# A linear-attention and two-MLP kernel on one core: when layer 1's weight sums and stores are issued, and the last eight attention chunks in halves of 64 tokens

## The chip, the cores and the metric

The kernel runs on one core of one Trainium2 chip. Times are device microseconds (us) of one execution. TensorE (PE in the profile) does the matrix products; VectorE (DVE) and ScalarE (ACT) do the arithmetic between them; SyncE (SP) issues nearly all DMA transfers, in the order in which they are written, on one queue. The metric is the median time over several runs.

## The reference, cut to what matters

Causal linear attention with a decay per head, then two MLPs without biases, all in float32:

```python
# q, k, v: (4, 8, 768, 64)
gamma = 1.0 - 2.0 ** (-5.0 - np.arange(H))
for t in range(S):
    state = gamma * state + einsum('bhd,bhe->bhde', k[:, :, t], v[:, :, t])
    y[:, :, t] = scale * einsum('bhd,bhde->bhe', q[:, :, t], state)
x = y.transpose(0, 2, 1, 3).reshape(3072, 512)
h = x @ w_in;  x = (h * sigmoid(1.702 * h)) @ w_out      # w_in (512, 2048)
h = x @ w_in2; out = (max(h, 0) + alpha * min(h, 0)) @ w_out2
```

## The kernel before, in words

**Precision.** A float32 product is made of three products of rounded parts. A tensor is split into a high part, rounded by a cast on ACT, and a low part, the remainder, subtracted on DVE (`g_split`, `piece_hi`/`piece_lo` at L223 to L229, `x_split`).

**Two stages.** The 3072 tokens make six blocks of 512, or 24 attention chunks of 128 (six chunks to a sequence). The first stage does blocks 0 and 1 through MLP layer 1 by plain products: 32 steps, each an `mlp_h` of 12 matmuls into `ph` (L661) and an `mlp_y` of 12 matmuls into `py` (L680) that stands one step later (LAG = 1), so the last two `mlp_y` follow each other. A step has two *slots*: slot 2s comes behind the `mlp_h` of step s, slot 2s + 1 behind the `mlp_y` that follows it. The second stage (slot 64, called `base`, and later) does everything else, layer 1 of blocks 2 to 5 and all of layer 2, with a scheme of seven products for a 2x2 block product: 280 `h_unit`s of 6 matmuls (`pa` and `pd`, L763) and 280 `y_chunk`s (L836). It needs sums and differences of weight blocks (s1 to s4) and of activation blocks. Slots of the second stage come behind every third or fourth `h_unit`.

**Jobs in slots.** Everything that isn't a step or a unit is a job with a slot, in the dictionary `jobs`; `run(slot)` issues what stands there. On this one stream of work lie:

- `conv_words`, `conv_f32`, `conv_hi`, `conv_lo`: a weight block, given as 64-bit words, becomes a high and a low part. Layer 1's blocks m = 10 to 31 come at slots 11 + 1.1 (m - 10).
- `store` (L251): writes the parts of a block of layer 1 to device memory, at slot 24 + 0.9 (m - 10) for m = 10 to 31.
- `conv_sums` (L264, four DVE instructions on L271) at the slots of `SUMS_IN` (w_in) and, by `slice_sums`, `SUMS_OUT` (w_out); one slot later `conv_split` (L301) casts each sum on ACT (L225), subtracts the rest on DVE (L229) and stores both.
- `x_prep`: blocks of x for the second stage, from slot 53 to 62.

**Attention.** Chunks 0 to 7 and 16 to 23 go whole: `att_scores` (L332) makes the 128x128 scores `sc`, DVE multiplies them by the decay mask (`a`), and one slot later `att_out` (L360) makes the output `px` and the state update `pu`; `att_state` folds `pu` into the running state `diag`, and `att_x_kept` (L434) writes the output's scaled form into the `xl` tiles. Chunks 8 to 15 go in halves of 64 tokens: `half_step(o, new)` (L528), at the slots 36, 38, to 52, makes the scores and state updates of chunk `new` and, between them, the output of chunk `o` from its own scores and from two states, that before the chunk (`hstate`) and that in its middle (`mid`). DVE then makes `a` (L543), `mid` and `hstate` (L557, L561, L562) and `xl` (L572). ACT scales `v` by the decay one slot ahead (`half_v_scale`, L471). Loads of chunks 14 and later come by `load_early` into tiles named `early`. Between the two forms `swap_state` (L459) copies the state by three DMAs, as the halves keep two heads of each pair the other way round.

**What sets the order.** Each engine runs its instructions in program order. The tile framework puts the DVE and ACT instructions of an `mlp_h` or half step ahead of waiting weight work (`tc.high_priority`), by its own estimate and not by what happens on the chip. Each SP DMA also waits for the one eight places ahead of it.

Of the kernel before, what the change touches and what calls it, by code (L numbers as in the profile page):

```python
# [8 lines left out]
F32 = mybir.dt.float32  # L9
# [6 lines left out]
ALU = mybir.AluOpType  # L16
# [3 lines left out]
P = 128  # L20
C = 128
# [9 lines left out]
BT = 512  # L31
NB = NT // BT
LEAD = 5
# [4 lines left out]
HG = 100  # L38
EARLY = (
    {},  # L40
# [3 lines left out]
)  # L44
# [14 lines left out]
AHEAD = 3  # L59
YLAG = 36  # L60
QORD = [(6, 7, 4, 5, 0, 1, 2, 3)] + [tuple(range(8))] * 4
SUMS_IN = (37, 41, 45, 49, 53, 56, 59, 62)
SUMS_OUT = (62, 64, 66, 68, 47, 51, 55, 58)
LOADED = 4
RESIDENT = (6, 7)
RINGED = range(8, 14)
LOADS = (-5, -3, -1, 1, 2, 3, 4, 5)
STORE_W = (24, 0.9)
ATT1 = 36
W2_ORDER = [("in", i) for i in range(6)] + [("out", i) for i in range(4)]  # L70
W2_ORDER += [("in", 6), ("in", 7)] + [("out", i) for i in range(4, 8)]
# [4 lines left out]
def tile_linear_attention_two_mlps(ctx: ExitStack, tc, qk, kv, w1, w2, consts, alpha, out):  # L76
# [9 lines left out]
    nc = tc.nc  # L86
# [9 lines left out]
    ps_y = pool("ps_y", 1, space=PS)  # L96
# [9 lines left out]
    decay_out = cst[:, NLEAD:].rearrange("p (n i) -> p n i", n=NP)  # L106
    alpha_sb = cpool.tile([P, NF], F32, name="alpha_sb")
    nalpha = cpool.tile([P, NF], F32, name="nalpha")
    diag = cpool.tile([P, NP, D], F32, name="diag")
    hstate = [cpool.tile([P, NP, D], F32, name=f"hstate{i}") for i in range(2)]  # L110
# [14 lines left out]
    def take(name, shape=(P, 512), dtype=F32):  # L125
        i = free.popleft()
        t = spool.tile(list(shape), dtype, tag=f"s{i}", name=name)
        home[id(t)] = (i, t)
        return t

    def give(*ts):
        for t in ts:
            free.append(home.pop(id(t))[0])
# [36 lines left out]
    early = {}  # L170
# [147 lines left out]
    def new_x(j):  # L318
        x_hi[j] = xpool.tile([P, NP, BT], F32R, tag=f"xhi{j}", name="xhi")
        x_lo[j] = xpool.tile([P, NP, BT], F32R, tag=f"xlo{j}", name="xlo")  # L320


    att, xl = {}, {}

    def att_psum(c, which, shape):
        early = EARLY[c] if c < BT // C else EARLY[1] if c >= 4 * BT // C else {}
        if which in early:
            tag = early[which]
            return (ps_h if tag == "h" else ps_y).tile(shape, F32, tag=tag, name=which)
        return ps_a.tile(shape, F32, tag="a", name=which)  # L330
# [71 lines left out]
    def att_state(c):  # L402
        first = c % CPB == 0
        att[c], pu = att[c]
        if pu is not None:
            src = pu
            if not first:
                src = take("t", (P, NP, D))
                nc.vector.tensor_tensor(out=src, in0=pu, in1=diag, op=ALU.add)
                give(src)  # L410
            dec = decay_c.unsqueeze(2).to_broadcast([P, NP, D])
            nc.vector.tensor_tensor(out=diag, in0=src, in1=dec, op=ALU.mult)

    def att_x(c):
        if c >= 2 * BT // C:
            att_x_kept(c)
            return
        x32 = take("x32", (P, NP, C))
        early_x = c == BT // C - 1
        banks = att[c][0] if early_x else att[c]  # L420
        for n in range(2):
            px = banks[n][:, :2 * C].rearrange("p (n i) -> p n i", n=2)
            with tc.high_priority(HG):
                nc.vector.tensor_tensor(out=x32[:, n::2, :], in0=px, in1=decay_out[:, n::2, :], op=ALU.mult)
        j, i = divmod(c, BT // C)
        cols = slice(i * C, (i + 1) * C)
        if i == 0:
            new_x(j)
        nc.scalar.copy(out=x_hi[j][:, :, cols], in_=x32)  # L429
        if early_x:  # L430
            att_state(c)
        att[c] = x32

    def att_x_kept(c):  # L434
        banks = att.pop(c)
        t, i = divmod(c % (2 * BT // C), BT // C)
        for k in range(2):
            for d in range(2):
                if i == 0:
                    xl[k, d, t] = take("xl")  # L440
                with tc.high_priority(HG):
                    nc.vector.tensor_tensor(
                        out=xl[k, d, t][:, i * C:(i + 1) * C], in0=banks[k][:, d * C:(d + 1) * C],
                        in1=decay_out[:, 2 * d + k, :], op=ALU.mult,
                    )

    def att_x_low(c):
        j, i = divmod(c, BT // C)
# [12 lines left out]
        for s in range(2):  # L461
            nc.sync.dma_start(out=out[ROWS[s], 0::2, :], in_=src[ROWS[1 - s], 0::2, :])

    def half_psum(which):
        return (ps_h if which == "sc" else ps_a).tile([P, 512], F32, tag="h" if which == "sc" else "a", name=which)

    def half_v_scale(c):
# [53 lines left out]
    def leave(kind, c):  # L521
        loaded.pop((kind, c))
        if c in early:
            give(*early[c][:2] if kind == "qk" else early[c][2:])
        else:
            done()

    def half_step(o, new):  # L528
        if o is not None:
            att["px", o] = half_psum("px")  # L530
        if new is not None:
            att["sc", new] = half_psum("sc")
            att["pu", new] = half_psum("pu")
        half_products(o, new)
        if o is not None:
            give(att.pop(("v", o)), att.pop(("a", o)), att.pop(("mid", o)))
            leave("qk", o)
        if new is not None:
            leave("kv", new)
        with tc.high_priority(HG):  # L540
            if new is not None:
                a = att["a", new] = take("a", (P, 2 * NP, HC))
                nc.vector.tensor_tensor(  # L543
                    out=a, in0=att.pop(("sc", new)).rearrange("p (n i) -> p n i", i=HC),
                    in1=half_causal.unsqueeze(1).to_broadcast([P, 2 * NP, HC]), op=ALU.mult,
                )
                half_state(new)
            if o is not None:
                half_x(o)
# [13 lines left out]

    def half_x(c):
        px = att.pop(("px", c)).rearrange("p (n i) -> p n i", n=NP)
        n = c - 2 * BT // C
        t, i = divmod(n, BT // C)
        for k in range(2):
            for d in range(2):
                if i == 0:  # L570
                    xl[k, d, t] = take("xl")
                nc.vector.tensor_tensor(  # L572
                    out=xl[k, d, t][:, i * C:(i + 1) * C], in0=px[:, 2 * d + k, :],
                    in1=decay_out[:, 2 * d + k, :], op=ALU.mult,
                )
# [319 lines left out]
    per = BT // C  # L895
# [3 lines left out]
    base = 2 * len(steps)  # L899
# [3 lines left out]
    def job(slot, fn, *args, load=()):  # L903
        jobs.setdefault(int(slot), []).append((fn, args, load))

    def attention(c, s_scores, s_out, s_x, s_low):
        if c < 4 * per:
            job(s_scores, att_scores, c, load=(("qk", c), ("kv", c)))
        else:
            job(LOADS[c - 4 * per] + base, load_early, c)  # L910
            job(s_scores, att_scores, c)
        job(s_out, att_out, c)
        job(s_x, att_x, c)
        if c < 2 * per:
            job(s_low, att_x_low, c)

    def convert(key, slot):
        job(slot, conv_words, key, load=(key,))
# [3 lines left out]
        if key[2] % 2 and (key[0] == "in" or key[1] == 2):  # L922
            i = key[2] // 2
            s = slot + 3 if key[1] == 2 else SUMS_IN[i]
            job(s, conv_sums, key[0], key[1], i)
            job(s + 1, conv_split, key[0], key[1], i)

    turn_at = {}
    for c in range(NCH):
        if 2 * per <= c < 4 * per:  # L930
            s = ATT1 + 2 * (c - 2 * per)
            turn_at.setdefault(s, {})["new"] = c
            turn_at.setdefault(s + 2, {})["o"] = c
            if c in RINGED:
                job(s - 1, half_v_scale, c, load=(("qk", c), ("kv", c)))
            else:
                job(s - 4, load_early, c)
                job(s - 1, half_v_scale, c)
            continue
        if c < per:  # L940
            s = 2 * c - 2 * per - 1
        elif c < 2 * per:
            s = 2 * (c - per)
        else:
            s = base + c - 4 * per
        attention(c, s, s + 1, s + 1, s + 2)
    for s, t in turn_at.items():
        job(s, half_step, t.get("o"), t.get("new"))
    job(2 * per + 4, swap_state, hstate[2 * per % 2], diag)
    job(ATT1 + 4 * per, swap_state, diag, hstate[4 * per % 2])  # L950
    for ft in range(NF):
        for n, kind in enumerate(("in", "out")):
            m = 2 * ft + n
            lead = 2 * LEAD
            convert((kind, 1, ft), m - 2 * per + CS if ft < LEAD else lead + 1 + 1.1 * (m - lead))
            kind, i = W2_ORDER[m // 2]
            convert((kind, 2, 2 * i + m % 2), base + W2_AT[m])
            job(12 + m if ft < LEAD else STORE_W[0] + STORE_W[1] * (m - 10), store, (("in", "out")[n], 1, ft))
    for i in range(NQ):
        if i < LOADED:  # L960
            job(SUMS_OUT[i] - 2, slice_load, i)
# [37 lines left out]
    o = NLEAD  # L999
# [172 lines left out]
```

## Time and profile before

| | before |
|---|---|
| runs, us | 1038.05, 1035.78, 1036.85 |
| median, us | 1036.85 |
| profiled execution, span us | 1037.7 |
| PE busy, share of the span | 1019.7 us, 98% |
| DVE busy | 873.8 us, 84% |
| ACT busy | 679.3 us, 65% |
| mean granted TensorE clock, share of full speed | 0.996 |

The profiled execution has no time of its own beside its span of 1037.7 us, from its first to its last instruction; the median of the runs is 0.85 us below it. Shares are averages over both stages. Matmuls are pipelined, so a matmul's duration is not the distance to the next one.

### The profile page before, as it was taken

What the parts mean: (1) busy time and instruction counts of PE and PEld (TensorE: products, weight loads), DVE (VectorE), ACT (ScalarE), POOL (GpSimd) and SP (SyncE); (2) the same over time, 40 slices, a digit from 0 to 9 for tenths busy, and PEclk for the clock granted to TensorE, in tenths of its full rate; (3) what the DMA queues carried; (4) which work ended last, traced back from release to release, by engine and by line L of the source; (5) the groups of instructions that cost most, each with busy time, mean ns of one, the idle gap of its engine ahead of it and who ended that gap; (6) DMA issues with size and microseconds to landing.
All of it is one profiled execution on the core that took longest, in us unless ns stands there. A gap on an engine that the chain in (4) does not pass through costs nothing.

```text
span 1037.7 us, 18658 instructions
## 1 busy us (share of the span) xinstructions
PE 1019.7 (98%) x6316; PEld 837.9 (81%) x6316; DVE 873.8 (84%) x1738; ACT 679.3 (65%) x1405; POOL 0.2 (0%) x4
## 2 busy tenths in 40 slices
PE   7999999898999999999999999999999999999998
PEld 5778888787888888888888888888888888888886
DVE  6999845997989999888899999998677978677792
ACT  6887835466776885765886776775555855556740
POOL 0000000000000000000000000000000000000000
PEclk9999999998999999999999999999999999999999
DMA  8689939689999889989989899896786766775671
GB/s 326 228 266 396 349 118 368 228 320 319 385 392 388 268 310 370 324 309 357 341 286 361 276 320 334 294 314 180 228 274 212 220 215 194 226 245 178 187 203 61
DMA packets 147231, 289.80 MB, mean 279 GB/s; under 512 B 17472, under 2 KB 17856, under 8 KB 147136
## 3 DMA queue, kind: packets, MB, share of 16 engines
q1 hardware_dynamic: 146848, 288.30, 80.8%
q8 instruction: 50, 0.82, 0.3%
q10 hardware_dynamic: 288, 0.31, 0.1%
q14 instruction: 45, 0.37, 0.1%
HBM read 213.83 MB, written 74.45 MB: 278 GB/s over the span
## 4 chain that ended last, share of the span: by engine, by line
PE 85%; DVE 8%; DMA 4%; ACT 1%; SPq 1%; issue 0%; DVEq 0%; ACTq 0%
PE py L836 37%; PE pa L763 21%; PE pd L763 16%; PE py L680 5%; PE ph L661 4%; DMA wcin<-wb 2%; DVE wb L229 1%; PE px L372 1%; DVE s L271 1%; PE sc L344 1%; DMA early<-kv 1%; DVE gl L645 1%; DMA ld<-kv 1%; DVE a L355 1%; DMA early<-qk 1%; DVE cvt L210 0%
## 5 line engine op out<-in xcount | busy, mean ns | idle before, releaser
L836 PE MATMUL py<-gh,yw 128*128 128x512 f32 x1120 | 299.5, 389 | 0.0
L836 PEld LDWEIGHTS py<-gh,yw 128*128 128x128 f32 x1120 | 210.2, 188 | 43.7
L763 PE MATMUL pa<-xo,hw 128*128 128x512 f32 x912 | 231.0, 390 | 0.0
L763 PEld LDWEIGHTS pa<-xo,hw 128*128 128x128 f32 x912 | 170.9, 188 | 35.8
L645 DVE TENSOR_TENSOR gl<-gw,gh 128x512 fp32r<-128x512 f32 x240 | 161.1, 687 | 42.9 <-ACT gh L644 36.9
L644 ACT CAST gh<-gw 128x512 fp32r<-128x512 f32 x240 | 145.7, 620 | 53.6 <-PE py L836 24.3
L763 PE MATMUL pd<-xo,hw 128*128 128x512 f32 x684 | 173.3, 389 | 0.0
L836 PE MATMUL py<-gl,yw 128*128 128x512 f32 x560 | 172.6, 389 | 0.0
L763 PEld LDWEIGHTS pd<-xo,hw 128*128 128x128 f32 x684 | 128.2, 188 | 26.8
L836 PEld LDWEIGHTS py<-gl,yw 128*128 128x128 f32 x560 | 105.1, 188 | 21.8
L850 DVE TENSOR_TENSOR yc<-py,yc 128x512 f32<-128x512 f32 x99 | 63.7, 684 | 26.2 <-PE py L836 26.2
L637 DVE SCALAR_TENSOR_TENSOR gw<-t,nalpha,gw 128x512 f32<-128x512 f32 x96 | 71.4, 748 | 15.5 <-ACT gw L636 15.3
L635 ACT ACTIVATE t<-gw 128x512 f32<-128x512 f32 x72 | 45.5, 632 | 52.7 <-DVE gw L778 49.8
L225 ACT CAST wb<-s 128x256 fp32r<-128x256 f32 x128 | 48.3, 402 | 41.4 <-DVE s L271 27.6
L680 PE MATMUL py<-gh,wb 128*128 128x512 f32 x256 | 67.3, 405 | 3.2 <-ACT gh L644 2.8
L661 PE MATMUL ph<-xhi,wb 128*128 128x512 f32 x256 | 64.2, 392 | 1.2 <-ACT xhi L429 1.2
L775 ACT COPY gw<-pa 128x512 f32<-128x512 f32 x80 | 46.8, 585 | 26.3 <-PE pa L763 25.7
L680 PEld LDWEIGHTS py<-gh,wb 128*128 128x128 f32 x256 | 47.9, 192 | 15.4 <-ACT gh L644 4.1
L661 PEld LDWEIGHTS ph<-xhi,wb 128*128 128x128 f32 x256 | 47.6, 188 | 11.6 <-ACT xhi L429 1.3
L778 DVE TENSOR_TENSOR gw<-pd,gw 128x512 f32<-128x512 f32 x80 | 54.8, 685 | 2.2 <-PE pd L763 2.1
L229 DVE TENSOR_TENSOR wb<-s,wb 128x256 fp32r<-128x256 f32 x128 | 50.0, 419 | 7.1 <-ACT wb L225 6.9
L799 DVE TENSOR_TENSOR gw<-gw 128x512 f32<-128x512 f32 x80 | 53.9, 688 | 0.3
(119 smaller groups left out, 1358.4 us busy)
## 6 DMA issues: line engine op xcount, KB each, us to landing
hw<-wcin SPq DMA_DIRECT2D x266, 256.0 KB, 4.7
yw<-wcout SPq DMA_DIRECT2D x232, 256.0 KB, 3.8
ld<-w SPq DMA_DIRECT2D x64, 512.0 KB, 5.9
wcin<-wb SPq DMA_DIRECT2D x112, 256.0 KB, 5.1
wcout<-wb SPq DMA_DIRECT2D x88, 256.0 KB, 4.2
yw<-wo SPq DMA_DIRECT2D x48, 256.0 KB, 5.1
wo<-wb SPq DMA_DIRECT2D x32, 256.0 KB, 6.3
early<-qk SPq DMA_DIRECT2D x26, 256.0 KB, 6.0
```

The source lines that it names most:

```text
L225: nc.scalar.copy(out=w[:, 0:256], in_=src)
L229: nc.vector.tensor_tensor(out=w[:, 256:], in0=src, in1=w[:, 0:256].bitcast(F32), op=ALU.subtract)
L637: nc.vector.scalar_tensor_tensor(out=g, in0=t, scalar=nalpha[:, ft:ft + 1], in1=g, op0=ALU.mult, op1=ALU.add)
L644: nc.scalar.copy(out=gh, in_=g)
L645: nc.vector.tensor_tensor(out=gl, in0=g, in1=gh.bitcast(F32), op=ALU.subtract)
L661: nc.tensor.matmul(out=ph, lhsT=cols(w, low, k), rhs=x[:, k, :], start=(n == 0), stop=(n == len(prods) - 1),)
L680: nc.tensor.matmul(out=py[e], lhsT=lhsT, rhs=g, start=(begin and seen[e] == 1), stop=(end and seen[e] == 3))
L763: nc.tensor.matmul(out=ps, lhsT=w[:, 256 * part_ + k * P:256 * part_ + (k + 1) * P], rhs=x[2 * k + low], start=(n in (0, 1, 3) and m == 0) ...
L778: nc.vector.tensor_tensor(out=g, in0=ps, in1=g, op=ALU.add)
L799: sub = lambda o, x, y: nc.vector.tensor_tensor(out=o, in0=x, in1=y, op=ALU.subtract)
L836: nc.tensor.matmul(out=ps[e], lhsT=w[:, at:at + P], rhs=t, start=(fresh and seen[e] == 1), stop=(m == GQ - 1 and seen[e] == 3), skip_group ...
L850: add_ = lambda o, x: nc.vector.tensor_tensor(out=o, in0=ps, in1=x, op=ALU.add)
```

## The change

`SUMS_IN` brings the eight `conv_sums` of w_in forward, from slots 37 to 62 to slots 33 to 51. A new `STORE_FAST` leaves the stores alone up to slot 31 and lets those behind it follow 0.4 slot apart instead of 0.9, so that the last comes at slot 36 and not 42. Chunks 16 to 23 go in halves too, by `half_step` at slots `base` to `base + 8`, one slot apart. In that stage the banks of `sc`, `pu` and `px` are those of `ps_y`, as the whole form had them. `att_x_kept`, the second `swap_state` and a use of `EARLY` go.

```diff
-SUMS_IN = (37, 41, 45, 49, 53, 56, 59, 62)
+SUMS_IN = (33, 35, 37, 39, 41, 44, 47, 51)
 SUMS_OUT = (62, 64, 66, 68, 47, 51, 55, 58)
 LOADS = (-5, -3, -1, 1, 2, 3, 4, 5)
 STORE_W = (24, 0.9)
+STORE_FAST = (31, 0.4)
...
 def att_x(c):
-        if c >= 2 * BT // C:
-            att_x_kept(c)
-            return
...
-    def half_psum(which):
+    def half_psum(which, c):
+        if c >= 4 * BT // C:
+            tag = {"sc": f"y{3 * (c % 2)}", "pu": "y1", "px": "y2"}[which]
+            return ps_y.tile([P, 512], F32, tag=tag, name=which)
         return (ps_h if which == "sc" else ps_a).tile([P, 512], F32, tag="h" if which == "sc" else "a", name=which)
...
+    def store_slot(m):
+        s = STORE_W[0] + STORE_W[1] * (m - 2 * LEAD)
+        late = max(0, s - STORE_FAST[0])
+        return min(s, STORE_FAST[0] + late * STORE_FAST[1] / STORE_W[1])
...
     for c in range(NCH):
-        if 2 * per <= c < 4 * per:
-            s = ATT1 + 2 * (c - 2 * per)
+        if c >= 2 * per:
+            late = c - 4 * per
+            s, after = (base + late, 1) if late >= 0 else (ATT1 + 2 * (c - 2 * per), 2)
             turn_at.setdefault(s, {})["new"] = c
-            turn_at.setdefault(s + 2, {})["o"] = c
+            turn_at.setdefault(s + after, {})["o"] = c
             if c in RINGED:
                 job(s - 1, half_v_scale, c, load=(("qk", c), ("kv", c)))
             else:
-                job(s - 4, load_early, c)
+                job(LOADS[late] + base if late >= 0 else s - 4, load_early, c)
                 job(s - 1, half_v_scale, c)
             continue
...
-    job(ATT1 + 4 * per, swap_state, diag, hstate[4 * per % 2])
...
-            job(12 + m if ft < LEAD else STORE_W[0] + STORE_W[1] * (m - 10), store, (("in", "out")[n], 1, ft))
+            job(12 + m if ft < LEAD else store_slot(m), store, (("in", "out")[n], 1, ft))
```

On DVE, the end of the first stage, before: from behind the third-last `gl` of the 32 steps to the last. `s_3344` and `s_3345` are sums of w_in, `s_3356` and `s_3357` of w_out (made from `wsum`).

```order
L271 TENSOR_TENSOR s_3344<-cvt 128x256
L271 TENSOR_TENSOR s_3345<-cvt 128x256
L271 TENSOR_TENSOR s_3344<-s_3344,cvt 128x256
L294 TENSOR_TENSOR wsum<-wo 128x256
L271 TENSOR_TENSOR s_3345<-cvt,s_3344 128x256
L294 TENSOR_TENSOR wsum<-wo 128x256 x2
L601 TENSOR_TENSOR t_3121<-xl,t_3121 128x512
L601 TENSOR_TENSOR t_3131<-xl,t_3131 128x512
L229 TENSOR_TENSOR wb<-s_3344,wb 128x256 x2
L229 TENSOR_TENSOR wb<-s_3345,wb 128x256 x2
L645 TENSOR_TENSOR gl<-g,gh 128x512
L294 TENSOR_TENSOR wsum<-wo 128x256
```

And in the changed kernel, the same place (lines L295, L272, L230 and L632 are what L294, L271, L229 and L645 were, and L576 what L589 was):

```order
L632 TENSOR_TENSOR gl<-g,gh 128x512
L295 TENSOR_TENSOR wsum<-wo 128x256 x3
L272 TENSOR_TENSOR s_3369<-wsum 128x256
L272 TENSOR_TENSOR s_3369<-s_3369,wsum 128x256
L230 TENSOR_TENSOR wb<-s_3369,wb 128x256
L272 TENSOR_TENSOR s_3370<-wsum,s_3369 128x256
L230 TENSOR_TENSOR wb<-s_3369,wb 128x256
L230 TENSOR_TENSOR wb<-s_3370,wb 128x256
L632 TENSOR_TENSOR gl<-g,gh 128x512
L576 TENSOR_TENSOR xo<-xl,xo 128x512 x2
L576 TENSOR_TENSOR xo<-t_3178,xo 128x512
L632 TENSOR_TENSOR gl<-g,gh 128x512
```

The sums of w_in made from `cvt` are gone from this place; the sum of w_out stands ahead of the second-last `gl` and no longer between it and the last.

On ACT, before, around the last activation `g` of the first stage; `wb` are the casts of the sum of w_out.

```order
L632 ACTIVATE g<-ph 128x512
L644 CAST gh<-g 128x512
L225 CAST wb<-s_3356 128x256
L225 CAST wb<-s_3357 128x256
L225 CAST wb<-s_3356 128x256
L225 CAST wb<-s_3357 128x256
L588 CAST xo<-xl 128x512 x2
L632 ACTIVATE g<-ph 128x512
L588 CAST xo<-t_3121 128x512
L644 CAST gh<-g 128x512
```

In the changed kernel, from the second-last `g` to the last:

```order
L619 ACTIVATE g<-ph 128x512
L631 CAST gh<-g 128x512
L459 ACTIVATE v<-early,cst 128x64 x8
L575 CAST xo<-xl 128x512 x2
L619 ACTIVATE g<-ph 128x512
L575 CAST xo<-t_3178 128x512
L631 CAST gh<-g 128x512
```

Ahead of the last `g` stand eight scalings of `v` (chunk 16) where four casts of sums stood.

On PE, the changed kernel's first two attention jobs of the second stage, the first with `new` alone, the second with both; the products of a line pair follow each other in turns, of which the first are shown.

```order
L750 MATMUL pd<-xo,wb 128x512 x12
L469 MATMUL sc<-early 64x64 x16
L469 MATMUL pu<-v,early 64x64 x16
L750 MATMUL pa<-xo,wb 128x512 x12
L750 MATMUL pd<-xo,wb 128x512 x6
L469 MATMUL px<-early,hstate_82 64x64
L469 MATMUL sc<-early 64x64
L469 MATMUL px<-early,hstate_82 64x64
```

Before, the row of `pd` x12 was followed by eight scores of 128x128, and the second job by the 24 or 32 products of `att_out` (x8 of 64x64 into `px` first) and the next chunk's scores. The units between them are the same ones in both kernels.

## Rows read from the trace of the kernel before

**Rows 1.** Timeline of PE, half steps without a wait: start, us, what.

```profile
139.93 1.15 PE L481 MATMUL sc<-ld 64*64 64x64 f32 x32
...
141.94 2.11 PE L680 MATMUL py<-gh,wb 128*128 128x512 f32 x8
...
147.61 0.27 PE L481 MATMUL px<-ld,hstate 64*64 64x64 f32 x1
...
149.63 1.66 PE L680 MATMUL py<-gh,wb 128*128 128x512 f32 x6
```

**Rows 2.** Timeline of PE, starts of the last three half steps and a pause.

```profile
187.11 0.24 PE L481 MATMUL px<-ld,hstate 64*64 64x64 f32 x1 [0.26 <-DVE hstate L561]
...
196.64 0.29 PE L481 MATMUL px<-early,hstate 64*64 64x64 f32 x2 [1.66 <-DVE hstate L561]
...
200.59 0.21 PE L481 MATMUL pu<-v,early 64*64 64x64 f32 x1 [1.85 <-issue]
...
206.52 0.68 PE L481 MATMUL px<-early,hstate 64*64 64x64 f32 x16
```

**Rows 3.** The chain that ended last: start, us, what; a transfer and two units.

```profile
179.41 7.37 DMA early<-kv
...
262.93 2.72 PE pa L763 x12
```

**Rows 4.** Timeline of PE, the end of the first stage.

```profile
235.93 1.98 PE L680 MATMUL py<-gh,wb 128*128 128x512 f32 x8
...
241.65 3.78 PE L680 MATMUL py<-gh,wb 128*128 128x512 f32 x8 [2.84 <-ACT gh L644]
...
246.94 3.29 PE L763 MATMUL pa<-xo,wb 128*128 128x512 f32 x12
250.06 2.88 PE L763 MATMUL pd<-xo,wb 128*128 128x512 f32 x12
```

**Rows 5.** Timeline of ACT at the same place.

```profile
237.29 1.13 ACT L225 CAST wb<-s 128x256 fp32r<-128x256 f32 x3 [3.06 <-DVE s L271]
...
240.98 0.61 ACT L644 CAST gh<-g 128x512 fp32r<-128x512 f32 x1
```

**Rows 6.** Windows: length, PE, PEld, DVE, ACT, POOL busy, PE clock, DMA share, GB/s.

```profile
130.00:140.00 10.00, 10.00 (x47) 8.01 (x47) 3.42 (x7) 4.26 (x13) 0.00 (x0) 1.00 0.00 0
...
190.00:200.00 10.00, 7.09 (x145) 5.82 (x144) 9.68 (x29) 3.90 (x10) 0.00 (x0) 1.00 0.69 236
...
230.00:240.00 10.00, 8.81 (x39) 6.95 (x37) 9.97 (x28) 5.05 (x13) 0.00 (x0) 1.00 0.96 329
240.00:250.00 10.00, 8.35 (x24) 6.67 (x25) 8.12 (x17) 8.02 (x28) 0.00 (x0) 0.66 0.71 239
...
280.00:290.00 10.00, 10.00 (x130) 8.12 (x130) 10.00 (x28) 7.54 (x20) 0.00 (x0) 1.00 1.04 381
```

**Rows 7.** Timeline of PE, whole chunks in the second stage: first two and last.

```profile
252.87 1.16 PE L344 MATMUL sc<-early 64*128 64x128 f32 x16
...
253.96 3.02 PE L763 MATMUL pa<-xo,wb 128*128 128x512 f32 x12
...
258.27 0.69 PE L372 MATMUL px<-v,early 128*64 128x64 f32 x16
...
261.27 0.96 PE L763 MATMUL pd<-xo,wb 128*128 128x512 f32 x3
...
315.40 0.96 PE L763 MATMUL pa<-xo,hw 128*128 128x512 f32 x3
```

**Rows 8.** Timeline of DVE: instructions that follow each other at once.

```profile
189.48 0.42 DVE L271 TENSOR_TENSOR s<-s,wsum 128x256 f32<-128x256 f32 x1
189.82 0.42 DVE L229 TENSOR_TENSOR wb<-s,wb 128x256 fp32r<-128x256 f32 x1
...
219.35 0.68 DVE L645 TENSOR_TENSOR gl<-g,gh 128x512 fp32r<-128x512 f32 x1
219.96 0.68 DVE L589 TENSOR_TENSOR xo<-t,xo 128x512 fp32r<-128x512 f32 x1
```

More of the change, by code (lines that the diff above doesn't have):

```diff
@@ L325, in att_psum @@
     def att_psum(c, which, shape):
-        early = EARLY[c] if c < BT // C else EARLY[1] if c >= 4 * BT // C else {}
+        early = EARLY[c] if c < BT // C else {}
         if which in early:
@@ L432, in att_x @@
         att[c] = x32
[L434 to L445, printed above, removed]
     def att_x_low(c):
@@ L529, in half_step @@
         if o is not None:
-            att["px", o] = half_psum("px")
+            att["px", o] = half_psum("px", o)
         if new is not None:
-            att["sc", new] = half_psum("sc")
-            att["pu", new] = half_psum("pu")
+            att["sc", new] = half_psum("sc", new)
+            att["pu", new] = half_psum("pu", new)
         half_products(o, new)
@@ L565, in half_x @@
         px = att.pop(("px", c)).rearrange("p (n i) -> p n i", n=NP)
-        n = c - 2 * BT // C
-        t, i = divmod(n, BT // C)
+        t, i = divmod(c % (2 * BT // C), BT // C)
         for k in range(2):
@@ L906, in attention @@
     def attention(c, s_scores, s_out, s_x, s_low):
[L907 to L911, printed above, removed]
+        job(s_scores, att_scores, c, load=(("qk", c), ("kv", c)))
         job(s_out, att_out, c)
         job(s_x, att_x, c)
-        if c < 2 * per:
-            job(s_low, att_x_low, c)
+        job(s_low, att_x_low, c)
     def convert(key, slot):
@@ L936, in tile_linear_attention_two_mlps @@
             else:
-                job(s - 4, load_early, c)
+                job(LOADS[late] + base if late >= 0 else s - 4, load_early, c)
                 job(s - 1, half_v_scale, c)
             continue
[L940 to L945, printed above, removed]
+        s = 2 * c - 2 * per - 1 if c < per else 2 * (c - per)
         attention(c, s, s + 1, s + 1, s + 2)
@@ L1140, in chosen @@
         n = np.arange(NCH)[:, None, None]
-        return np.where((n >= 2 * BT // C) & (n < 4 * BT // C), half, whole)
+        return np.where(n >= 2 * BT // C, half, whole)
     def weights(w_in, w_out, swap):
```

## The prediction

> **What bounds the kernel now.** The busy times of the page come first: PE is busy 98% of the span, so a gain must be PE work that goes away or a gap on PE that closes. The list of PE's waits and the windows say where the gaps are. In the second stage there are none worth naming: PE is busy 10.00 us of 10, though DVE is full there too (window 280 to 290) [rows 6]. The gaps lie between 180 and 250 us, at the end of the first stage, where DVE is busy 9.68 and 9.97 of 10 and PE 7.09 and 8.81 [rows 6]. The timeline of PE then gives each gap its place.
>
> A half step that waits for nothing takes 2.01 to 2.02 us to the next matmul (139.93 to 141.94, 147.61 to 149.63), and the distance to the next half step is 147.61 - 139.93 = 7.68 us [rows 1]. Eight such distances would put the ninth half step at 139.93 + 61.44 = 201.37. It starts at 206.52 [rows 2]: **5.15 us** are lost. Of these 1.85 lie between 187.11 and 196.64 (mostly the wait of 1.66 for `hstate`), 2.20 between 196.64 and 206.52 (a pause of 1.85 whose releaser the profile does not name), and 1.10 ahead of 187.11 [rows 2], where the chain runs through a late load of keys and values, 7.37 us from issue to landing [rows 3].
>
> The last `mlp_y` waits **2.84 us** for `gh` [rows 4]. `gh` is cast at 240.98, behind an ACT that had itself been waiting 3.06 us for sums of DVE [rows 5]: four casts of a sum stand ahead of the last `g` in ACT's order. So a DVE that is late with weight work holds the one PE step that has no other work to put in front. [...] Twelve matmuls from 241.65 to 246.94 take 5.29 us and the next twelve 3.12 (to 250.06), where the chain has 2.72 for twelve at the full clock [rows 3]. The clock costs 2.57 + 0.40 = **2.97 us** [rows 4].
>
> **The change part by part.**
>
> *Sums of w_in earlier.* Nothing is added or removed. One sum with its split is eight DVE instructions of 128x256, which follow each other 0.34 us apart (0.60 for 128x512) [rows 8]: 2.7 us, eight times. I counted the DVE instructions of both orders between one `gl` and the next with these spacings (narrower ones by width, an estimate). From the `gl` of step 26 to that of step 31, that is five steps of 5.44 us (twice 2.72 [rows 3]) or 27.2 us, DVE has 30.1 us to do before and 22.1 after: three sums left this stretch, at slots 56, 59 and 62. In the half steps' stretch, four gls from step 22 to step 26 (30.8 us), it has 34.1 before and 31.6 after. Carried forward from step to step (work less 7.69 or 5.44, never under zero), DVE's lag grows before to 2.4 us at step 25, 4.4 at 26 and 7.3 at 31; after it is 2.2 at step 23, 0.7 at 25 and 26, at most 2.8 at 27, and 0 at step 30. Before, PE begins to wait for `hstate` when that lag passes about 2.4. So I expect the last wait of 2.84 to go, and with it the fall of the clock, since PE is then busy without a break as it is everywhere else at 1.00: **5.8 us**. Of the 5.15 at the half steps the lag explains 1.85 and some of the rest.
>
> *Stores faster.* The same 256 KB transfers, sooner. The DMA share is 0.00 in the window 130 to 140 [rows 6], and SP's queue is in order: a store that is written early there no longer stands ahead of the early loads of chunks 14 and 15, the last of which landed 7.37 us after its issue [rows 3]. This works on the 1.10 us ahead of 187.11. If it doesn't help it costs nothing, since the early window is empty.
>
> *Halves for chunks 16 to 23.* The nine inserts of whole chunks into the units take, start to next unit, 1.09 (252.87 to 253.96), 3.00 (258.27 to 261.27) five times, 2.53, 2.56, and 1.44 for the last, which ends at 315.40 [rows 7]: 22.6 us. Nine half steps at 2.02 [rows 1] are 18.2. PE saves **4.4 us**. DVE's work is about the same: a half step has one 128x512, three 128x256 and four 128x128 instructions, a whole chunk two, two and four. ACT scales eight pieces of `v` either way. The three DMAs of the second `swap_state` and their wait for `hstate` go. [...]
>
> *What the halves may newly wait for.* A half step now comes three or four units, 4.08 or 5.44 us, behind the last one (a unit is half of 2.72), and needs `hstate` with its first product and the single bank `px` free. DVE's four instructions up to `hstate` take 0.60 + 3 x 0.34 = 1.6 us and the four `xl` about 0.8 more, 2.4 of at least 4.08. That leaves 1.7 us for other DVE work in between, on an engine that is full there [rows 6]. The whole form had a chain of about this length over the same one slot and PE didn't wait, but its state was needed behind eight or sixteen other products and its scores came last, which gave it some 2 us more. From below this costs nothing; from above the half steps at slots 48 and 50, 1.66 of wait for `hstate` each [rows 2], at three of the eight steps, 5 us. I take 1.5.
>
> *Sum.* 5.15 + 2.84 + 2.97 + 4.4 = 15.4 us is what could go. I leave 1.5 us of the half steps' 5.15 in place (nothing says that the pause of 1.85 goes; bounds 0 and 3) and 1.5 for the new ones (bounds 0 and 5). 15.4 - 3 = 12.4, and the profiled span of 1037.7 becomes 1025.3. The median of the runs is 0.85 under that span, so I predict **1024.5 us**.
>
> **The rivals.**
>
> *DVE is only full earlier* (12%). Five sums now fall into slots 44 to 52 (w_in at 44, 47, 51, w_out at 47, 51) where four did. The half steps then wait as before, and perhaps the last `gh` too. For it: 31.6 us of work in 30.8. Against: the lag that I count is under 3 us everywhere. With all of the 5.15 kept it gives 1024.5 + 3.65 = 1028; with the last wait and its clock kept too, 1034, and only the halves' 4.4 less the 1.5 remain.
>
> *The halves stall in the second stage* (9%), the one that ends on the other side. `hstate` or `px` comes late because weight conversions stand ahead of it on DVE. The place is PE's first product of the steps at `base + 2` to `base + 7`. At 1.66 + 1.85 = 3.5 us for each of seven steps, as at the step of 196.64 [rows 2], it is 24.6 us against a gain of 13.9 without them: about 1047. It turns the sign when the mean stall passes 13.9 / 7 = 2.0 us. For it: DVE at 10.00 of 10 [rows 6]. Against: whole chunks with nearly the same chain have no wait there.
>
> *A load or a scaling is late* (10%). The values of chunk 23 are loaded behind stores that wait for their splits, and its scaling stands on ACT ahead of a copy of `pd` that frees a bank. One such stall of 3 us with a fall of the clock behind it, 2.97 as after the last `mlp_y` [rows 4], gives 1024.5 + 6 = 1030.5.
>
> [...]
>
> **How the numbers follow.** The forecast has 67%: 1020 (all gaps closed, 1037.7 - 15.4 - 0.85 = 1021.5, and a little of DVE's lag in the second stage) to 1029 (both bounds at the upper end: 1024.5 + 1.5 + 3.5 = 1029.5). The range of 8 in 10 takes in the late load and half of the first rival: 1020.5 to 1031.5. A run of this kernel tells 0.2%, 2.1 us, from no change. Faster than 1034.8 are the forecast and nearly all of the rivals but the second: 0.88. Slower than 1038.9 is the stall in the second stage, above all: 0.07. Between them 0.05.
>
> **What would show it.** The changed profile should have no wait of `py` for `gh` of more than 0.5 us at the end of the first stage, a granted clock of 1.00 in every window from 130 us on, and the unit behind the last `mlp_y` at about 235 to 237 us and not 246.94. The half steps of the second stage should be 2.0 us long, to the next unit. DVE should reach 9 of 10 earlier, from about 165 us, and have room from 220 to 240. Waits for `hstate` at `base + 2` and later, or a clock under 1.00 behind one, would make the prediction wrong, and so would a wait for `gh` that has only moved to an earlier step.

## The result, and the profile after

The changed kernel is **slower**: 1043.28 us (median of six runs, 1040.67 to 1050.24) against 1036.48 before (six runs, 1035.20 to 1038.05), a ratio of 1.0070 with a 95% interval of 1.0053 to 1.0087. The forecast was 1024.5 and a gain. The profiled execution took 1042.88 us with a span of 1041.1, 3.4 us more than the span before.

The waits of PE over the span come first (engine, line, what it waited for: total us, times, longest).

```profile
PE pu L469 <- issue: 7.2, 4, 2.5
PE px L469 <- DVE hstate L549: 2.0, 1, 2.0
...
PE px L469 <- DVE xl L559: 1.4, 2, 0.7
```

The wait of the last `py` for `gh`, 2.84 us before [rows 4], is no longer among them. In its place is one that nothing releases as far as the profile shows ("issue"), 7.2 us in four pieces. Before, there was one such piece, of 1.85 [rows 2]. The timeline of PE at the end of the first stage shows what the forecast had right:

```profile
238.42 1.98 PE L667 MATMUL py<-gh,wb 128*128 128x512 f32 x8
240.23 1.07 PE L667 MATMUL py<-gl,wb 128*128 128x512 f32 x4
241.14 1.98 PE L667 MATMUL py<-gh,wb 128*128 128x512 f32 x8
242.95 1.07 PE L667 MATMUL py<-gl,wb 128*128 128x512 f32 x4
243.86 2.88 PE L750 MATMUL pa<-xo,wb 128*128 128x512 f32 x12
```

The last two `mlp_y` follow each other 2.72 us apart without a gap. Before, 241.65 to 246.94 were spent on the last alone [rows 4]. But the first unit starts at 243.86, only 3.08 us sooner. The timeline of the half steps at slots 48 and 50 says where the rest went:

```profile
187.56 0.29 PE L469 MATMUL px<-ld,hstate 64*64 64x64 f32 x2 [1.96 <-DVE hstate L549]
190.65 2.74 PE L667 MATMUL py<-gh,wb 128*128 128x512 f32 x8
...
201.53 0.21 PE L469 MATMUL pu<-v,early 64*64 64x64 f32 x1 [2.50 <-issue]
201.80 3.41 PE L667 MATMUL py<-gh,wb 128*128 128x512 f32 x8
```

The wait at slot 48 was 0.26 and is 1.96; the pause at slot 50 was 1.85 and is 2.50 [rows 2]. By the starts of the half steps (138.96 for the first, 209.07 for the ninth; 61.44 without waits) this stretch now loses 8.67 us, and lost 5.15. Part of that is the clock, granted at 0.50 for 3.4 us behind each of the two gaps: the eight matmuls behind the two gaps take 2.74 and 3.41 us, and eight behind a half step without a wait 2.11 [rows 1]. In the second stage, where PE had waited for nothing, there are gaps in five of the nine half steps (timeline of PE, starts of half steps and first instructions behind a pause):

```profile
279.46 0.32 PE L469 MATMUL px<-early,hstate 64*64 64x64 f32 x2 [0.96 <-DVE s L272]
283.72 0.27 PE L469 MATMUL pu<-v,early 64*64 64x64 f32 x1 [2.06 <-issue]
283.92 4.60 PE L750 MATMUL pa<-xo,hw 128*128 128x512 f32 x12
288.36 1.54 PE L750 MATMUL pd<-xo,hw 128*128 128x512 f32 x6
...
292.74 0.27 PE L469 MATMUL pu<-v,early 64*64 64x64 f32 x1 [1.07 <-issue]
...
301.90 0.27 PE L469 MATMUL pu<-v,early 64*64 64x64 f32 x1 [1.60 <-issue]
...
307.79 0.30 PE L469 MATMUL px<-early,hstate 64*64 64x64 f32 x2 [0.61 <-DVE xl L559]
```

And the clock, by windows of 10 us (length, PE, PEld, DVE, ACT, POOL busy, clock, DMA share, GB/s):

```profile
180.00:190.00 10.00, 7.91 (x138) 6.33 (x140) 9.29 (x26) 4.67 (x15) 0.00 (x0) 0.93 0.89 323
190.00:200.00 10.00, 9.03 (x171) 7.38 (x165) 8.75 (x25) 5.95 (x18) 0.00 (x0) 0.90 0.84 279
200.00:210.00 10.00, 8.47 (x61) 6.72 (x62) 7.98 (x24) 2.96 (x7) 0.00 (x0) 0.83 0.88 323
...
230.00:240.00 10.00, 10.00 (x45) 8.26 (x44) 5.21 (x13) 6.54 (x18) 0.00 (x0) 1.00 0.99 339
...
280.00:290.00 10.00, 7.94 (x140) 6.30 (x136) 5.36 (x15) 5.57 (x17) 0.00 (x0) 0.83 0.95 322
```

The fall of the clock at the end of the first stage (0.66 in one window [rows 6]) is gone; three others have come, at 188.6, 202.3 and 284.2, each behind a gap in PE's work (1.96, 2.50 and 2.06 us). Twelve matmuls at 283.92 take 4.44 us, to 288.36, instead of 2.72.

The balance of the two profiled executions, by the starts of the same matmuls: 0.97 us gained ahead of the first half step; 2.11 from there to the first unit (5.6 behind the ninth half step, where 34.79 us stand against 40.42, less 3.5 at the half steps); 5.30 lost from there to the end of the last attention job (243.86 to 317.62 against 246.94 to 315.40); 1.2 lost later. Together 3.4.

**The pauses named issue.** Between them stand as many PE instructions as one counts here (windows cut at the ends of the pauses):

```profile
201.53:283.72 82.19, 78.42 (x889) 64.63 (x889) 67.23 (x166) 49.17 (x126) 0.00 (x0) 0.98 0.91 317
283.72:292.74 9.02, 7.95 (x126) 6.31 (x126) 2.73 (x8) 3.49 (x11) 0.00 (x0) 0.81 0.98 322
292.74:301.90 9.16, 7.56 (x125) 6.11 (x125) 5.68 (x14) 6.86 (x17) 0.00 (x0) 1.00 1.04 382
```

Matmuls and weight loads are 889 + 889, 126 + 126 and 125 + 125. With the semaphore instructions of the same engine, which a window doesn't count, they are 1792, 256 and 256, that is 7 x 256, 256 and 256. The page lists an instruction queue whose packets are 16 KB (0.88 MB in 54), 50 of them before:

```profile
q8 instruction: 54, 0.88, 0.3%
```

54 x 256 = 13824, and PE has 6700 matmuls, 6700 weight loads and 366 others, 13766; before it is 50 x 256 = 12800 against 12993, so the count holds to within one block. So, by these counts, PE's own code comes in blocks of 256 instructions, on a queue beside that of the data (q8; q1 moves 288.17 MB). The packet that belongs to the pause at slot 50 started at 199.24 and landed at 200.20; PE went on at 201.53, 1.33 us later. From 130 us on, 14 of the kernels of this study have such pauses, in 21 places of 0.8 us or more: 20 named issue in the lists of PE's waits, and one of 3.43 us in `e10_loads` that the profile puts down to ACT. In the two traces of the kernel before and the changed one, all five of these pauses ended 1.24 to 1.45 us after a packet of this queue had landed (1.24 at 200.59 before; 1.33, 1.45, 1.36 and 1.32 in the changed kernel). One more wait of the changed kernel at a block's end, of 0.96 us up to 279.46, was ended by a DVE instruction, 4.89 us after the last packet, and is not counted. At four of the 54 blocks the crossing cost 1.07 to 2.50 us; at the others PE's waits have no pause named issue.

### The profile page after: what moved, and what is told of

Its sections match the earlier page's. It is cut to its first block, busy times and chain, and to the rows that moved or that the text cites. A ratio compares the mean times of both kernels' runs of the same rounds, so it can differ in the third digit from the quotient of the medians.

```text
span 1041.1 us, 19420 instructions
## 1 busy us (share of the span) xinstructions
PE 1017.7 (98%) x6700; PEld 836.6 (80%) x6700; DVE 871.5 (84%) x1738; ACT 674.9 (65%) x1406; POOL 0.2 (0%) x4
## 3 DMA queue, kind: packets, MB, share of 16 engines
q1 hardware_dynamic: 146288, 288.17, 81.1%
## 5 line engine op out<-in xcount | busy, mean ns | idle before, releaser
L632 DVE TENSOR_TENSOR gl<-gw,gh 128x512 fp32r<-128x512 f32 x240 | 160.6, 685 | 45.2 <-ACT gh L631 39.5
L230 DVE TENSOR_TENSOR wb<-s,wb 128x256 fp32r<-128x256 f32 x128 | 50.1, 418 | 7.8 <-ACT wb L226 7.4
```

The lines of the kernel that those rows point to most:

```text
L230: nc.vector.tensor_tensor(out=w[:, 256:], in0=src, in1=w[:, 0:256].bitcast(F32), op=ALU.subtract)
L632: nc.vector.tensor_tensor(out=gl, in0=g, in1=gh.bitcast(F32), op=ALU.subtract)
```

## The experiments

Two theories stood at first. **A**: the halves use up PE's instructions faster than they come. A full half step is 128 matmuls and 128 weight loads, one block, in 2.02 us; at twelve matmuls in 2.72 us, PE's other work takes 29 us for as many (an estimate from the row of 2.72). **B**: the moved sums make DVE late, and the unnamed pauses are waits for DVE or ACT. Ratios are to runs of the kernel before on the same chip, with 95% intervals.

### The change in two parts

`e1_sums_stores` is the kernel before with the new `SUMS_IN` and `store_slot`; `e2_halves` is the changed kernel with both put back.

```diff
 e2_halves, against the changed kernel:
-SUMS_IN = (33, 35, 37, 39, 41, 44, 47, 51)
+SUMS_IN = (37, 41, 45, 49, 53, 56, 59, 62)
-STORE_FAST = (31, 0.4)
+STORE_FAST = (31, 0.9)
```

> The sums and the stores of the change, with chunks 16 to 23 whole as before. Theory A (PE's own instructions come too slowly for the halves: the pauses named issue in the second stage stand exactly 256 PE instructions apart, or a multiple of it, and end 1.3 us after a 16 KB packet of the instruction queue has landed): no pause in the second stage, one of about 2.5 us left in the half step at slot 50, the first unit near 244 us as in the changed kernel, and 1036.5 - 3.1 = 1033.4 us. Theory B (the moved sums make DVE late, and the pauses are waits for DVE or ACT that the profile does not name): slower than before, about 1040, with pauses at the same places.

> The halves of the change alone, sums and stores at the old slots. Theory A: the second stage of the changed kernel with its pauses, three or four of 1 to 2.5 us 256 PE instructions apart, and the old end of the first stage: 1036.5 + 5.3 = 1041.8 us, less about 3 if the clock does not fall behind the pauses. Theory B: no pauses in the second stage, since DVE is as before: 1036.5 - 4.4 = 1032.1 us.

Sums and stores alone: 1039.4 us, ratio 1.0019 (1.0007 to 1.0032). Halves alone: 1040.83, 1.0035 (1.0022 to 1.0049). Both parts are slower, and their sum, 0.54%, is most of the 0.7% of the change. The halves went as A had it in time (1041.8 expected). There is no pause named issue in the second stage of `e1_sums_stores`. In `e2_halves` A expected three or four of 1 to 2.5 us; there is one large one, at the fifth half step, one PE instruction behind the place in the changed kernel, with 6.8 us of the lower clock behind it, and a small one of 0.36 later:

```profile
286.21 0.76 PE L750 MATMUL pa<-xo,hw 128*128 128x512 f32 x1 [4.12 <-issue]
```

The sums and stores were a miss for A, which expected a gain of 3. B had the loss and nearly the time (1040), but not its pauses in the second stage. PE's and ACT's waits from 170 to 205 us in `e1_sums_stores`:

```profile
PE px L482 <- DVE hstate L562: 3.7, 1, 3.7
PE pu L482 <- issue: 2.5, 1, 2.5
...
ACT wb L226 <- DVE s L272: 9.8, 4, 4.7
ACT wb L226 <- DMA wcin<-wb: 3.5, 1, 3.5
```

The half step at slot 48 waits 3.7 us for `hstate`. DVE's instructions for it stand behind a subtraction of a weight sum, that behind a cast on ACT, and the cast waits 3.5 us for a store of weights to land, whose tile it takes over.

This lateness eats the gain, but it is not the whole of the loss. In this profiled execution (span 1039.5) the first unit starts at 245.41, 1.5 us sooner than before, as 1.2 are gained ahead of the first half step and 5.6 at the end of the stage, and the half steps lose 10.48 us instead of 5.15. From there to the end of the last attention job it takes 70.6 us (68.5 before), and 1.2 us more after that.

### The code stream moved by 128 instructions

`e3_shift` is the changed kernel with 64 products of 8 columns more at its start.

```diff
         nc.tensor.matmul(out=idle, lhsT=warm[:, :P], rhs=warm, start=True, stop=True)
+    for _ in range(64):
+        nc.tensor.matmul(out=idle[:, :8], lhsT=warm[:, :P], rhs=warm[:, :8], start=True, stop=True)
```

> The changed kernel with 64 tiny products of 8 columns more at its start, while PE waits for its first load, so that every later PE instruction stands 128 places further on. Theory A: the pauses move 128 instructions towards the front, that is about half a half step, or to other half steps, and still stand 256 apart; the time moves with them by some us either way, 1038 to 1047. Theory B: they stay at the same instruction of the same half step, near the last state update, and the time is that of the changed kernel, 1043 plus at most 1.

It took 1045.36 us, 1.0080 (1.0057 to 1.0104). The pause at slot 50 is gone (that half step takes 2.23 us, and 4.84 in the changed kernel), and no pause named issue is left in the second stage. That is A. But the time is not better: the seventh full half step there waits 6.4 us for DVE's `xl`. Ahead of it ACT waited 6.26 us for a load of keys and values and DVE 3.68 for a store. The timeline of PE:

```profile
304.94 0.33 PE L469 MATMUL px<-early,hstate 64*64 64x64 f32 x1 [6.37 <-DVE xl L559]
```

### Half as many PE instructions in the half steps

`e4_bf16` reads the upper 16 bits of the operands of the last eight chunks' products, which leaves their low bits out; `e7_bf16_twice` issues each of those products twice.

```diff
+            if (o or new) >= 4 * BT // C:
+                lhsT, rhs = lhsT.bitcast(BF16)[:, 1::2], rhs.bitcast(BF16)[:, 1::2]
-            nc.tensor.matmul(
+            for _ in range(2 if (o or new) >= 4 * BT // C else 1):   # e7 only
+                nc.tensor.matmul(
```

> The changed kernel with the products of the last eight chunks on the upper 16 bits of their operands (bf16), which leaves out their low bits: each product is one pass and not two, 64 PE instruction pairs a half step and not 128. Theory A: no pause in the second stage and half steps of 1.0 to 1.6 us, so 7.2 us of pauses and falls of the clock less in that stage beside 4 to 8 us of PE work: about 1043 - 10 - 5 = 1028. Theory B: DVE's and ACT's work is the same and comes sooner after the last step, so the pauses stay or grow: 1038 or more.

> The bf16 form of the last eight chunks with each of their products issued twice, so that accumulated ones count twice: the same operands, DVE and ACT work and transfers as with bf16 once, but again 128 PE instruction pairs a half step. Theory A (code supply): pauses named issue come back in the second stage, three or more of 1 to 2.5 us, 256 instructions apart, and the time is 1026.5 + 9 x 0.63 + about 6 of pauses and clock = 1038. Theory B (it was the width or the passes of the operands): no pauses, half steps of 1.27 us, 1026.5 + 5.7 = 1032.

Once: 1026.47 us, 0.9894 (0.9875 to 0.9914), no pause named issue in the second stage, half steps of 0.64 us. That is what A expected (1028), though PE's time per half step fell too. Twice: 1036.47, 0.9995 (0.9980 to 1.0010), between the 1038 of A and the 1032 of B. The three pauses that A expected did **not** come, and the half steps take 1.27 us, both as B had it. PE waited 3.6 us for `xl` at the fourth half step; that the next blocks had time to land during this wait is my guess and was not shown. So the number of instructions alone doesn't make a pause. That it hangs on the place in the code is shown by the kernels whose stream is moved, not by this one.

### Sums and stores apart

> The moved sums alone: whole chunks, stores at the old slots. Theory A1 (the sums at slots 41 to 51 put their splits' stores into the stretch 150 to 205 us, where the DMA engines are full; ACT then waits for a store to give its tile back, DVE waits for ACT's cast, and the half steps at slots 48 and 50 for hstate): slower than before, about 1039 as with sums and stores together, PE's waits for hstate 3 us or more, ACT's wait for wcin<-wb 2 us or more near 186 us. Rival B1 (the faster stores crowd the queue, the sums are a gain): faster than before by the 5.8 us of the end of the first stage, about 1031.

> The faster stores alone: whole chunks, sums at the old slots. Theory A1: they only move transfers from the full stretch into an empty one; same or faster than before, 1034 to 1036.5, the wait of the last mlp_y for gh still there (1.5 to 3 us). Rival B1: slower than before, 1039 or more, with longer waits at slots 46 to 50.

The sums alone (`SUMS_IN` new, stores as before): 1039.31 us, 1.0011 (1.0002 to 1.0021). The stores alone: 1037.11, 0.9995 (0.9983 to 1.0007). The stores change nothing that can be measured, and the sums are the slower part of the two. The wait for `hstate` in `e5_sums` was smaller than expected (1.6 us in three pieces), and ACT waited there for loads of keys and values (5.8 and 4.5 us) rather than for stores; the theory had the right stretch and only one of its queues.

`e8_sums_apart` keeps whole chunks and the faster stores and takes the sums out of slots 44 to 52 (against `e1_sums_stores`):

```diff
-SUMS_IN = (33, 35, 37, 39, 41, 44, 47, 51)
+SUMS_IN = (32, 34, 36, 38, 40, 42, 56, 60)
```

> Whole chunks, the faster stores, and the sums of w_in at slots 32, 34, 36, 38, 40, 42, 56, 60: ahead of and behind the stretch of slots 44 to 52, not in it. Theory A1: waits for hstate under 1 us, one code pause of 2 to 2.5 us left at slot 50, no wait of the last mlp_y and no fall of the clock there: 1036.5 - 2.84 - 2.97 - 1.5 = 1029.2 us, 1028 to 1033. Rival B1, or DVE's lag as the cause whatever the DMA does: 1034 or more.

It took **1033.58 us, 0.9952 (0.9936 to 0.9968)**, faster than both kernels, though a little above the 1028 to 1033 that was expected. Its half steps wait for no DVE instruction, the pause at slot 50 is 0.83 us, and the first unit starts at 236.40, 10.5 us sooner than before. The timeline of PE there:

```profile
195.38 0.21 PE L482 MATMUL pu<-v,early 64*64 64x64 f32 x1 [0.83 <-issue]
...
233.55 2.11 PE L681 MATMUL py<-gh,wb 128*128 128x512 f32 x8
235.50 1.07 PE L681 MATMUL py<-gl,wb 128*128 128x512 f32 x4
236.40 2.88 PE L764 MATMUL pa<-xo,wb 128*128 128x512 f32 x12
```

That profiled execution (span 1027.5) is among the faster ones of a kernel whose runs went from 1029.27 to 1035.67.

### The halves on top of it, their loads, and the shift once more

`e9_apart_halves` is the changed kernel with the sums of `e8_sums_apart`; `e10_loads` has `LOADS = (-6, -4, -2, 0, 1, 2, 3, 4)` besides, `e11_loads_shift` the 64 tiny products too. `e12_apart_shift` is `e8_sums_apart` with the tiny products.

> The whole change with the sums of w_in at slots 32, 34, 36, 38, 40, 42, 56, 60. If the costs of the sums and of the halves add up: the first stage of the kernel with whole chunks and these sums, and the halves' loss of 4.3 us behind it, 1033.6 + 4.3 = 1038. If the halves lost only because the first stage was late: 1033.6 - 4.4 = 1029.

> As before it, and each early load of chunks 16 to 23 one slot earlier. Theory C (the halves scale v one slot sooner than the whole form, the loads were left where they were, so ACT waits 6 to 8 us in all for keys and values, and what stands behind on ACT and DVE is late for PE): ACT's waits for early<-kv fall under 2 us, the waits of the half steps for xl and hstate in the second stage go, and the time falls by 2 to 4 us against the kernel with the loads where they were. Theory A alone (code supply): no change, within 1 us.

> The same with 64 tiny products at the start, 128 PE instructions further on. Theory A: the pause named issue at slot 50 and those of the second stage move or go, 2 to 6 us less or other steps hit, with the tiny products costing up to 2 us at the start. If the pauses have nothing to do with the position in the instruction stream: they stay at the same half steps, and the time is the same or 1 to 2 us more.

> Whole chunks, the faster stores, the sums apart, and the 64 tiny products at the start. Theory A: no pause in the half step at slot 50, where all eight other kernels with two full passes have one of 0.8 to 2.5 us at the same PE instruction, and a time of 1033.6 - 1.5 = 1032, plus up to 2 for the start. If the pause is a wait for DVE or ACT: it stays.

With the halves: 1037.48 us, 1.0001 (0.9991 to 1.0010), where 1038 was expected if the two add up. So it is not the late first stage that spoils the halves. The loads one slot earlier: 1039.91, 1.0025 (1.0015 to 1.0036), 2.4 us more, where theory C (late loads of keys and values hold up ACT, and so DVE and PE) expected 2 to 4 less. ACT's waits for keys and values from 245 to 320 us, first in `e9_apart_halves`, then in `e10_loads`:

```profile
ACT v L459 <- DMA early<-kv: 1.4, 1, 1.4
...
ACT v L459 <- DMA early<-kv: 1.5, 1, 1.5
```

In the changed kernel they were 6.2 us. They had gone with the sums already, so `e10_loads` took nothing away and is no test of C. `e9_apart_halves` is: with 1.4 us of these waits the halves still cost 0.5% against `e8_sums_apart`. Shifted, the pair took 1041.10 (1.0039, 1.0023 to 1.0056) and 1036.85 (0.9998, 0.9986 to 1.0010). In both the pause at slot 50 is gone. In `e12_apart_shift` (timeline of PE, first instruction of that half step and the next big matmul):

```profile
197.16 0.27 PE L482 MATMUL px<-early,hstate 64*64 64x64 f32 x1
...
199.18 1.19 PE L681 MATMUL py<-gh,wb 128*128 128x512 f32 x4
```

2.02 us, and 3.2 to 5.0 in every kernel with the stream as it was. The time did not follow (at most 1034 was expected). The first half step begins at 142.70, and at 138.63 without the tiny products, and the last `mlp_y` waits 1.51 us for `gh`, which it doesn't in `e8_sums_apart`.

### Transfers, or work; and the second stage alone

`e13_stores_late` and `e14_apart_late` are `e1_sums_stores` and `e8_sums_apart` with the stores of the last two sums of w_in, whose tiles stay in SBUF for the second stage, ten and three slots behind the sums. `e15_shift_base` is `e9_apart_halves` with the 64 tiny products between the two stages.

```diff
-                put(wc[kind, layer, i][W_AT[kind][name] + n], w)
+                if (kind, layer) != ("in", 1) or i not in RESIDENT:
+                    put(wc[kind, layer, i][W_AT[kind][name] + n], w)
...
+    for i in RESIDENT:
+        job(SUMS_IN[i] + PUT_LATE, put_resident, i)
```

> Sums and faster stores as in the change, whole chunks, and the stores of the last two sums of w_in (slots 47 and 51), whose tiles stay in SBUF anyway, ten slots later. DVE and ACT do the same work at the same slots; sixteen 256 KB... eight transfers of 256 KB leave the stretch 185 to 205 us. Theory A1 (the transfers make the half steps late, through tiles that come free late): the waits of the steps at slots 48 and 50 for hstate fall from 3.7 to under 2 us and the time from 1039.4 to 1036 or less. Theory L (DVE's and ACT's work at those slots is the cause, whatever the transfers do): 1038.5 to 1040, waits as before.

> Whole chunks, faster stores, sums of w_in at 32, 34, 36, 38, 40, 42, 56, 60, and the stores of the last two three slots later than their splits. Theory A1: 0 to 2 us less than with the stores at once (1033.6), as the queue is less full at the turn to the second stage. Theory L: no change.

> [...] Theory A: the pause named issue at the end of the fifth half step of the second stage (2.8 us and a fall of the clock behind it, at the same PE instruction in four kernels) goes or moves; that of slot 50 in the first stage stays; time 1037.5 + 2.3 - 4.5 = 1035.3. If the second-stage pause hangs on DVE, ACT or loads: it stays at the fifth half step, and the time is 1039.8.

`e13_stores_late`: 1036.92 us, 0.9999 (0.9988 to 1.0009), where the stores at once had 1.0019 (1.0007 to 1.0032); that lies between the two theories. ACT's and PE's waits from 170 to 205 us:

```profile
PE px L489 <- DVE hstate L569: 2.5, 2, 1.3
...
ACT wb L227 <- DMA wcin<-wb: 1.0, 1, 1.0
```

ACT waits 1.0 us for a store and not 3.5, PE 2.5 for `hstate` and not 3.7. By the starts of the first and the ninth half step the stretch loses 6.23 us (139.19, 206.86), 10.48 with the stores at once (138.70, 210.62) and 1.27 with the sums apart (138.63, 201.34). So these two sums' stores are nearly half of what the moved sums cost there. Whether the rest is DVE's and ACT's own work at those slots or the stores of the other six sums was not tried. `e14_apart_late`: 1032.66, 0.9956 (0.9943 to 0.9970), no different from `e8_sums_apart` in what these runs can tell.

`e15_shift_base`: 1037.78, 1.0007 (0.9994 to 1.0020), between the 1035.3 of A and the 1039.8 against it. Timelines of PE at the fifth half step of the second stage, first in `e9_apart_halves`:

```profile
273.70 0.27 PE L469 MATMUL px<-early,hstate 64*64 64x64 f32 x1
...
278.63 0.21 PE L469 MATMUL pu<-v,early 64*64 64x64 f32 x1 [2.84 <-issue]
278.77 0.56 PE L750 MATMUL pa<-xo,hw 128*128 128x512 f32 x1
```

and with the stream moved:

```profile
278.72 0.27 PE L469 MATMUL px<-early,hstate 64*64 64x64 f32 x1
...
280.74 0.50 PE L750 MATMUL pa<-xo,hw 128*128 128x512 f32 x1
```

5.07 us become 2.02. The pause of the first stage, whose code did not move, is still there (1.31). So the second-stage pause is the code stream too. The time is the same all the same. In these two profiled executions the stretch from the first unit to the end of the last attention job falls from 72.20 to 69.77 us, though the half step ahead of the pause waits longer for `xl`, the one bank of `px` (2.62, and 1.80 without the shift). The tiny products cost 1.61 us (239.36 to 240.97), where the expected times add 2.3, which no run shows, and 2.4 us are lost behind the stretch (723.1 and 725.5 us to the end of the span), 1.71 of them in one wait for ACT at 318.20.

## Why the prediction was wrong

- **The end of the first stage** was right: no wait for `gh`, no fall of the clock there, 5.6 us where the forecast had 5.8.
- **The 5.15 us at the half steps** was the first step that failed. I left 1.5 of it in place; 8.67 were lost. By the starts these are 2.45 ahead of slot 48 (the wait for `hstate`), 2.82 in the half step with the pause, and about 3.3 at the lower clock behind the two (1.72 from 187.56 to 196.96, 1.61 from 201.80 to 209.07). The lag that I counted added DVE's work and took every operand to be there in time. The sums at slots 41 to 51 have ACT casts and stores behind them, in a stretch where the DMA engines are busy 0.83 to 0.97, and DVE stands in order behind a cast that waits for a store (1.7 us here, 3.5 in `e1_sums_stores`). The first rival named the place (five sums at slots 44 to 52) and was given 12%, but counted it as a lag of under 3 us.
- **"Nothing says that the pause of 1.85 goes"** was the sentence to stop at. It was PE's code. At this block's end PE stood still for 2.50 us in the changed kernel and went on 1.33 us after the next block had landed. I took the half step's 128 products for 2.02 us of PE and never counted them as instructions.
- **The halves' new waits** were the second step that failed, mis-sized: 1.5 us, bound 5; by the trace of the changed kernel they are 10.2. Of these 5.7 are code (2.44, 1.39 and 1.87 us over 2.02 at 279.46, 289.83 and 298.91), 2.8 waits for DVE, and 1.7 the clock behind them. Against them the saving of 4.4 us of PE's time is real: half steps without a wait take 2.01 to 2.02 there too. But no kernel with halves collects it. Whole chunks without a wait take 68.06 us from the first unit to the end of the last attention job (`e8_sums_apart`, 236.40 to 304.46); with halves it is 72.2 to 73.8 with the code's pauses and 69.77 to 75.69 in the three kernels whose moved stream is rid of all but one of 0.35 us. The rival on the other side (9%) had the place, the second stage, and the sign, but a wait for `hstate` as its mechanism, which is the smaller part. It put the turn of the sign at a mean stall of 2.0 us over seven steps; 10.2 us are 1.5 a step, and the sign turned because the first stage lost too.
- **The late load or scaling** (10%) is there, 6.2 us of ACT's waits in the second stage, but the halves cost as much with 1.4 (`e9_apart_halves`).
- **The stores** cost and gain nothing (`e6_stores`).
- **The 2.02 us of a half step** held: 128 products of 64x64 start 15.8 ns apart in the changed kernel too. The 64 tiny products of `e15_shift_base`, with 128x128 weights, start 25 ns apart (1.61 us for 64).

What stays open: why the waits for `xl` in the second stage grow as soon as a code pause is taken away (`e3_shift`, `e15_shift_base`). In `e3_shift` ACT stood 6.26 us behind a load and DVE 3.68 behind a store there, and the DMA engines are busy 0.95 and 1.03 in the changed kernel (280 to 300), but no run here took one of these transfers away. So the pauses are shown to be the code's, but no run shows what the whole kernel would gain without them. Open as well is a loss that the prediction doesn't have: behind the last attention job the span lasts another 722.2 to 722.3 us in the three kernels with the sums at their old slots and 723.0 to 724.9 in those with moved sums and the stream as it was (the bf16 kernels aside).

## What to carry to other kernels

Count the instructions of a rewrite as well as its microseconds: where one engine issues a few hundred small instructions in some us, its own code has to come in that time (here 256 of PE's in 2.02 us, 16 KB, with the DMA engines at 0.83 to 1.04), and a pause that no semaphore explains, at a multiple of 256 instructions as here, is worth checking for that. Work that is moved out of a full stretch has to land in an empty one for every queue that it uses, the stores behind it too: the same eight sums were a loss at slots 33 to 51 and a gain of 0.5% at slots 32 to 42, 56 and 60. And an engine's unexplained pause in the profile before is a cost that may come again (1.85 us before, 2.50 after), not noise.

## What the runs showed of the hardware

The transfer of a 16 KB block of code takes 0.88 to 1.14 us in the first 390 us of the changed kernel, but it came late: the blocks at 290.42 and 299.62 started 6.7 and 6.9 us after PE had begun on the one before, with the DMA engines at 0.98 and 1.04. The pause at slot 50 was built up step by step. With the block ends counted back from that pause, PE still had 274 instructions to go to a block when its transfer started at 141.31 us, and 223, 176, 147, 93, 70, 54 and 0 at the next seven transfers, up to 199.24. Why they didn't start sooner stays open.

And a gap of about 2 to 2.5 us in PE's work was followed by 3.4 us at a granted clock of 0.50 in the changed kernel (from 188.6, 202.3 and 284.2), but not each time: the same pause before, of 1.85 us behind a wait of 1.66, had none, and neither had a pause of 2.61 us up to 200.93 in `e13_stores_late` (window, with the clock behind the five busy times):

```profile
200.00:210.00 10.00, 9.07 (x99) 7.53 (x99) 9.56 (x29) 2.88 (x7) 0.00 (x0) 1.00 0.46 163
```
